# Operands of sixteen groups made over the MLP instead of twelve, in a fused attention, MLP and experts kernel

## The chip, the cores and the metric

The kernel runs on one core of a Trainium2 chip. The metric is the device time of one execution in microseconds (us); the time given for a kernel is the median of its runs.

## The reference, cut to what matters

```python
# attention, 4 batches x 8 heads x 576 x 64: x is 2304 tokens x 512
q_s = exp(q - max(q, -1)); q_s /= sum(q_s, -1)
k_s = exp(k - max(k, 2));  k_s /= sum(k_s, 2)
x = einsum(q_s, einsum(k_s, v))
# MLP, w_in 512 x 2048, w_out 2048 x 512
h = x @ w_in
x = maximum(0.01 * h, h) @ w_out
# gate
logits = x @ w_gate                    # 2304 x 8
P = exp(logits - logits.max())
for _ in range(8):                     # "balance"
    P /= P.sum(1, keepdims=True) + 1e-09
    P /= P.sum(0, keepdims=True) + 1e-09
    P *= N / E
# 8 experts, w1 512 x 1024, w2 1024 x 512 each
for e in range(8):
    out += P[:, e:e+1] * (maximum(x @ w1[e], 0) @ w2[e])
```

## The kernel before, in words

**Three stages.** Attention comes first, the MLP next (to some 499.5 us), then the experts. Every float32 operand is split in a high and a low part of type fp32r: `split` (L535, L536) casts the high part on ACT and subtracts it from the original on DVE, so each product is three matmuls, and PE carries nearly all of the time. Helper `mm` (L203) issues every matmul, so PE's rows are told apart by tile, not by line.

**The MLP** runs through 16 units of 128 hidden columns in 4 phases of 4 units; in a phase it takes 6 blocks of 384 tokens. A step is two half-steps: `first` (12 matmuls of 384 columns and the activation) and `second` (adds into the four banks y0 to y3, which are evicted at the end of a block by ACT, L239, or DVE, L241). There are 192 half-steps.

**The experts** run 3 superblocks of 768 tokens; in each, 32 groups of two 128-column units of the 8 experts' hidden layers (`NQ` = 32, `NG` = 96 in all). A group has seven half-steps t0 to t6 (`group`), one for each of the seven products with which Strassen's scheme replaces eight: banks `pa`, `pb`, `pc`, `pd` on PE, sums on ACT (L1000, L1025, L1027) and DVE (L944). The second matmul of groups 0 to `N0`-1 of superblock 0 is ordinary: `y_tile`, three tiles of 12 matmuls of 512 columns, tiles `e<-wb_t,xs`. All other groups do it by Strassen as well: `y_pass`, seven products of 6 matmuls of 384 columns, tiles `e<-xs,wb_t` and `e<-wa,wb_t`, with sums on ACT, POOL (L839, L840) and DVE (L845).

**Operands.** Strassen's scheme needs sums and differences of weight quarters, each split in high and low. Groups 0 to `N0`-1 make theirs while they run (`pair_sums` on POOL, `pair_w1` on ACT and DVE), and keep them in DRAM for the two later superblocks (`keep_w1` L559, `keep` L569: SP queue). Groups from `N0` on need theirs in DRAM before they start (`ring_load` L725 brings them in). Those are made during the MLP by `early_load` and `early_op`: list `early` holds two makings per pair of groups (w1 and w2), and `EARLY` names the half-step of each. One making: a load of 512 KB; two ACT casts; two DVE subtractions (L1206), of 128x768 and 128x1024 numbers; four POOL sums; stores of 768 and 1024 KB.

**Gate and balance.** In phase 4 of the MLP the finished blocks are transposed, split (`xs<-acc`, L364, L365) and multiplied with w_gate (tile `pg`). `balance` runs beside groups 0 to 5 of the experts: eight iterations, each with row sums and column sums on DVE, one tiny matmul with a matrix of ones (`pcs`) that adds the column sums over the partitions, a reciprocal `rc` (L423) and a scaling on DVE. `side_bank` gives `pcs` one of the banks y0 to y3, in turn.

**Borders.** At groups 32 and 64 a new superblock starts: its tokens need seven operands (`x_ahead`: four POOL subtractions of 128x768; `x_next`: splits). The output of a superblock is combined and transposed by `y_out` (tile `po`, copies L917, stores L919), which borrows banks; at the last superblock this is the end of the kernel. `op_split` makes the operands of the second matmul from the raw hidden activations, and each `sub_raw` one difference of them.

**What sets the order.** PE, ACT, POOL and SP run in the order in which the program issues (DVE's order is chosen by a scheduler). A generator's `yield` puts the rest of a task into the next half-step, `yield PE_NEXT` after that half-step's matmuls; `at(t, f)` starts a task at half-step t; `rest.append` puts a split at the start of the next half-step.

## Time and profile before

| | |
|---|---|
| median of 3 runs | 1960.81 us (1960.09 to 1961.35) |
| profiled execution, own time | 1959.87 us |
| its span | 1958.1 us |
| mean granted clock of TensorE | 0.994 |
| busy share of the span | PE 98%, PEld 95%, DVE 79%, ACT 43%, POOL 39% |
| DMA | 483.60 MB, mean 247 GB/s |

The span is the stretch of the profile from the first instruction to the last. PE is the matmul part of TensorE, PEld its weight loads (which lie beside the matmuls), DVE is VectorE, POOL is GpSimd, SP the engine whose queue starts most DMAs. Times in rows are in us from the start of the span, unless ns is said; `xN` is a count.

### The profile page before, as it was taken

Reading aid. Unit: us, or ns where it says so; the run is one execution under the profiler, and the core shown is the slowest. Engines: PE = TensorE matmul, PEld = TensorE weight load, DVE = VectorE, ACT = ScalarE, POOL = GpSimd, SP = SyncE. Lnnn points to the kernel's source line nnn. Section 1 sums busy time; section 2 is a strip of 40 time slices with the busy share of each in tenths; the row PEclk is TensorE's granted clock in tenths of the full one; section 3 lists DMA queues with packets and bytes.
Section 4 is the critical chain, followed back from the end, with each engine's and each line's share of the span. In section 5 each row is a group of like instructions: output and inputs, shape, how many; then the busy total and the mean of one; then the engine's idle time right before and its main releaser. Section 6 shows DMA issues by size and latency. Waiting matters only on the chain.

```text
span 1958.1 us, 31243 instructions
## 1 busy us (share of the span) xinstructions
PE 1925.3 (98%) x10835; PEld 1863.9 (95%) x10835; DVE 1550.6 (79%) x2285; ACT 836.5 (43%) x1528; POOL 758.5 (39%) x560
## 2 busy tenths in 40 slices
PE   7999999999999999999999999999999999999998
PEld 6999999999889999899999999999999999999998
DVE  7765768756788787779896898798898888888886
ACT  6744444444544444343344333333344433333333
POOL 4124323123323343126434445445633444544543
PEclk8999999999999999999999999999999999999999
DMA  6402768657688979888788988888888888887884
GB/s 249 166 14 67 248 205 272 209 175 236 244 282 286 325 285 331 286 315 258 233 276 262 326 275 260 270 261 260 254 256 247 275 261 261 259 260 235 278 260 153
DMA packets 279611, 483.60 MB, mean 247 GB/s; under 512 B 23536, under 2 KB 62848, under 8 KB 279424
## 3 DMA queue, kind: packets, MB, share of 16 engines
q1 hardware_dynamic: 278656, 480.04, 74.7%
q0 software_dynamic: 800, 1.57, 0.4%
q8 instruction: 88, 1.44, 0.3%
q14 instruction: 67, 0.55, 0.1%
HBM read 356.14 MB, written 128.52 MB: 248 GB/s over the span
## 4 chain that ended last, share of the span: by engine, by line
PE 62%; DVE 7%; issue 1%; ACT 1%; DMA 0%; SPq 0%; DVEq 0%; ACTq 0%
PE e L203 32%; PE pa L203 9%; PE pc L203 9%; PE pd L203 9%; PE pb L203 4%; DVE xs L536 1%; DVE c L944 1%; DVE mo_t L816 1%; DVE mo_t L802 1%; DVE wa L536 1%; DVE acc L845 1%; DMA mo_t<-in_w 0%; PE po L914 0%; ACT wa L535 0%; ACT acc L917 0%
## 5 line engine op out<-in xcount | busy, mean ns | idle before, releaser
L840 POOL TENSOR_TENSOR acc<-acc,acc 128x384 f32<-128x384 f32 x222 | 341.8, 1539 | 331.2 <-ACT acc L839 319.6
L203 PE MATMUL e<-xs,wb_t 128*128 128x384 f32 x1644 | 310.1, 334 | 1.4 <-ACT acc L917 1.4
L203 PE MATMUL e<-wa,wb_t 128*128 128x384 f32 x1548 | 290.5, 334 | 1.0 <-issue 0.9
L203 PEld LDWEIGHTS e<-xs,wb_t 128*128 128x128 f32 x1644 | 286.9, 188 | 2.3 <-ACT acc L917 2.2
L203 PEld LDWEIGHTS e<-wa,wb_t 128*128 128x128 f32 x1548 | 270.2, 188 | 1.5 <-issue 1.2
L816 POOL TENSOR_TENSOR mo_t<-mo_t 128x768 f32<-128x768 f32 x72 | 139.8, 1942 | 299.3 <-DVE mo_t L802 276.1
L839 ACT COPY acc<-e 128x384 f32<-128x384 f32 x222 | 106.3, 482 | 298.3 <-PE e L203 298.3
L536 DVE TENSOR_TENSOR wa<-mo_t,wa 128x768 fp32r<-128x768 f32 (+2 forms) x183 | 197.6, 1097 | 23.0 <-ACT wa L535 23.0
L203 PE MATMUL pa<-xs,wb_t 128*128 128x384 f32 x888 | 181.6, 339 | 3.0 <-ACT c L1000 2.9
L535 ACT CAST wa<-mo_t 128x768 fp32r<-128x768 f32 (+2 forms) x183 | 149.0, 839 | 79.0 <-DVE mo_t L816 57.2
L536 DVE TENSOR_TENSOR xs<-mo_t,xs 128x768 fp32r<-128x768 f32 x138 | 164.9, 1204 | 22.3 <-ACT xs L535 22.3
L203 PE MATMUL pc<-xs,wb_t 128*128 128x384 f32 x888 | 177.9, 334 | 1.5 <-ACT c L1025 1.5
L203 PE MATMUL pd<-xs,wb_t 128*128 128x384 f32 x888 | 178.4, 335 | 0.0
L845 DVE TENSOR_TENSOR acc<-e,acc 128x384 f32<-128x384 f32 x284 | 146.6, 548 | 34.8 <-PE e L203 19.8
L203 PE MATMUL e<-wb_t,xs 128*128 128x512 f32 x720 | 169.7, 393 | 1.2 <-DVE rc L423 1.2
L203 PEld LDWEIGHTS e<-wb_t,xs 128*128 128x128 f32 x720 | 135.7, 189 | 29.1 <-DVE rc L423 1.3
L203 PEld LDWEIGHTS pa<-xs,wb_t 128*128 128x128 f32 x888 | 154.1, 188 | 9.5 <-ACT c L1000 8.8
L535 ACT CAST xs<-mo_t 128x768 fp32r<-128x768 f32 x138 | 112.4, 836 | 109.8 <-DVE mo_t L816 70.3
L203 PEld LDWEIGHTS pc<-xs,wb_t 128*128 128x128 f32 x888 | 156.0, 188 | 2.1 <-ACT c L1025 2.1
L203 PEld LDWEIGHTS pd<-xs,wb_t 128*128 128x128 f32 x888 | 155.8, 188 | 0.3 <-DVE c L944 0.3
L816 DVE TENSOR_TENSOR mo_t<-mo_t 128x768 f32<-128x768 f32 x80 | 143.7, 1797 | 0.0
L802 DVE SCALAR_TENSOR_TENSOR mo_t<-c,mo_t 128x768 f32<-128x768 f32 (+1 forms) x152 | 126.6, 856 | 2.3
(178 smaller groups left out, 3226.9 us busy)
## 6 DMA issues: line engine op xcount, KB each, us to landing
wb_t<-d SPq DMA_DIRECT2D x1050, 256.0 KB, 3.4
d<-wa SPq DMA_DIRECT2D x20, 1792.0 KB, 9.9
d<-wb_t SPq DMA_DIRECT2D x56, 512.0 KB, 4.4
mo_t<-in_w SPq DMA_DIRECT2D x40, 512.0 KB, 7.4
raw<-in_wm SPq DMA_DIRECT2D x32, 512.0 KB, 5.4
d<-wa SPq DMA_DIRECT2D x15, 1024.0 KB, 5.1
d<-xs SPq DMA_DIRECT2D x13, 768.0 KB, 4.9
d<-wb_t SPq DMA_DIRECT2D x9, 1024.0 KB, 5.0
```

The source lines that it names most:

```text
L203: nc.tensor.matmul(o, a, b, start=start, stop=stop, **more)
L535: nc.scalar.copy(hi, a)
L536: return lambda: nc.vector.tensor_tensor(lo, a, r32(hi), op=ALU.subtract)
L802: nc.vector.scalar_tensor_tensor(o, p, 0.0, r, op0=ALU.max, op1=ALU.mult)
L816: eng.tensor_tensor(raw_q(o), raw_q(x), raw_q(y), op=ALU.subtract)
L839: nc.scalar.copy(t, bk[b])
L840: nc.gpsimd.tensor_tensor(c22, c22, t, op=ALU.add)
L845: return nc.vector.tensor_tensor(a, bk[b], a, op=ALU.add)
L944: add = lambda o, x, y: nc.vector.tensor_tensor(o, x, y, op=ALU.add)
```

## The change

`N0` falls from 20 to 16. Groups 16 to 19 of superblock 0 thereby take their operands from DRAM and do their second matmul by `y_pass`; 8 more makings run during the MLP (`EARLY` has 32 entries instead of 24: 11, 11 and 10 in phases 2, 3 and 4 instead of 8 each; in phase 4 they stand beside the half-steps after the gate's splits). With it:

- `side_bank` takes a bank that the running group's `y_tile` doesn't use, and `balance` issues some of its column sums later or earlier (`pcs4` one y tile later).
- The keeping of group 0's operands (`keep_w1(0)`, a DMA of 1792 KB) is issued at half-step `END`-3, not at the first half-step of group 0.
- `x_ahead`'s four POOL subtractions are issued one per two groups, from group `NQ`-8 on, not one after the other at `NQ`-6.
- At borders the splits `T3`, `B21`, `B22`, `T4` and a difference are issued one half-step later each; at the end `B11`, `T1`, `T2`, `T3` are placed anew in groups 94 to 96.
- `y_out` transposes in 4 banks of three tiles with copies of 384 columns and two DMAs of 384 rows each behind the last product, instead of 6 banks of two tiles with copies of 256 and one DMA each.

```diff
@@ -193,11 +193,11 @@
 
-    side_n = [0]
+    side_n = [0, 0]
 
...
         side_n[0] += 1
-        return ps_y.tile([P, 512], F32, tag=f"y{side_n[0] % 4}", name=name)
+        return ps_y.tile([P, 512], F32, tag=f"y{3 - side_n[1]}", name=name)
 
@@ -414,7 +414,7 @@
             yield
-            for _ in range((0, 2, 1)[min(it, 2)]):
+            for _ in range((0, 2, 1, 1, 2, 0, 1, 1)[it]):
                 yield
@@ -452,7 +452,7 @@
     NG = NSB * NQ
-    N0 = 20
+    N0 = 16
     KP = N0 // 2
@@ -664,7 +664,7 @@
     def stage_y(sb, n):
-        return acc[2 * NSB - 1 if sb == 0 else 1][:, n % 6 * 2 * P : (n % 6 + 1) * 2 * P]
+        return acc[2 * NSB - 1 if sb == 0 else 1][:, n * BLK : (n + 1) * BLK]
 
@@ -675,13 +675,8 @@
         x_parts[sb] = {"B11": b11, "T2": t2, "T1": t1, "T3": b12, "B21": b21, "B22": b22, "T4": t4}
-        nc.gpsimd.tensor_tensor(t1, b12, b11, op=ALU.subtract)
-        yield
-        nc.gpsimd.tensor_tensor(t2, b22, t1, op=ALU.subtract)
-        yield
-        nc.gpsimd.tensor_tensor(t4, b21, t2, op=ALU.subtract)
-        yield
-        nc.gpsimd.tensor_tensor(b12, b22, b12, op=ALU.subtract)
+        sub = lambda o, x, y: lambda: nc.gpsimd.tensor_tensor(o, x, y, op=ALU.subtract) and None
+        return sub(t1, b12, b11), sub(t2, b22, t1), sub(t4, b21, t2), sub(b12, b22, b12)
 
@@ -904,22 +899,24 @@
             yield
-        for th, quads in enumerate(((c11, cc), (dd, c22))):
+        for n, (a, th, h) in enumerate(((c11, 0, 0), (c22, 1, 1), (cc, 0, 1), (dd, 1, 0))):
+            if n % 2 == 0:
+                yield PE_NEXT
+            if sb == NSB - 1:
+                pt = bank(f"po{sb}_{dt}_{n}")[:, :BLK]
+            else:
+                pt = ps_y.tile([P, 512], F32, tag=f"y{(0, 2, 1, 3)[n]}", name=f"po{sb}_{dt}_{n}")[:, :BLK]
             for t in range(TB):
-                tt = th * TB + t
-                if tt % 2 == 0 and (tt < 4 or sb == NSB - 1):
-                    yield PE_NEXT
-                pt = (bank if sb == NSB - 1 else side_bank)(f"po{sb}_{dt}_{tt}")[:, : 2 * P]
-                for h, a in enumerate(quads):
-                    nc.tensor.transpose(pt[:, h * P : (h + 1) * P], a[:, t * P : (t + 1) * P], ident)
-                n = dt * 2 * TB + tt
-                o = stage_y(sb, n)
-                nc.scalar.copy(o, pt)
-                tok = 2 * sb * TB + tt
-                nc.sync.dma_start(
-                    (out if sb else ys_)[tok * P : (tok + 1) * P, :].rearrange("p (h t n) -> p h t n", h=2, t=2)[:, :, dt],
-                    o.rearrange("p (h n) -> p h n", h=2),
-                )
+                ts = slice(t * P, (t + 1) * P)
+                nc.tensor.transpose(pt[:, ts], a[:, ts], ident)
+            o = stage_y(sb, n)
+            nc.scalar.copy(o, pt)
+            tok = (2 * sb + th) * TB
+            k = 2 * h + dt
+            nc.sync.dma_start(
+                (out if sb else ys_)[tok * P : (tok + TB) * P, k * P : (k + 1) * P].rearrange("(t p) n -> p t n", p=P),
+                o.rearrange("p (t n) -> p t n", n=P),
+            )
 
@@ -988,11 +985,8 @@
                 y_steps(0)
-                if i == NG:
-                    rest.append(op_split(LG, "T3", raw_q(1)))
-                    rest.append(op_split(LG, "T2", raw_q(0)))
                 return
-            if i < N0 - 1:
+            if 0 < i < N0 - 1:
                 keep_w1(i)
@@ -1002,9 +996,6 @@
                 second_ops(0)
-            if ends(i - 1):
-                rest.append(op_split(eg - 1, "T3", raw_q(1)))
-                rest.append(op_split(eg - 1, "B21", raw_q(2)))
 
@@ -1030,12 +1021,16 @@
                 rest.append(op_split(eg, "T1", raw_q(0)))
+            if i == NG - 1:
+                rest.append(op_split(eg, "B11", raw_q(0)))
+            if ends(i - 1):
+                rest.append(op_split(eg - 1, "T3", raw_q(1)))
+                rest.append(op_split(eg - 1, "B21", raw_q(2)))
+
+        def t2():
+            drain()
             if ends(i - 1):
                 sub_raw(nc.vector, 2, 0, 2)
-                rest.append(op_split(eg - 1, "B22", raw_q(3)))
-
-        def t2():
-            drain()
             if i == N0:
@@ -1054,8 +1049,9 @@
             if ends(i - 1):
-                rest.append(op_split(eg - 1, "T4", raw_q(2)))
+                rest.append(op_split(eg - 1, "B22", raw_q(3)))
             if i == NG - 1:
+                sub_raw(nc.vector, 0, 1, 0)
                 rest.append(op_split(eg, "T1", raw_q(0)))
@@ -1081,6 +1077,8 @@
                 keep_w1(i)
+            if ends(i - 1):
+                rest.append(op_split(eg - 1, "T4", raw_q(2)))
 
@@ -1094,7 +1092,8 @@
                 if half == 0:
-                    rest.append(op_split(eg, "B11", raw_q(0)))
+                    if i < NG - 2:
+                        rest.append(op_split(eg, "B11", raw_q(0)))
                 elif not ends(i) and i < NG - 1:
@@ -1107,7 +1106,8 @@
                 if half == 0:
-                    sub_raw(nc.gpsimd if i < NG - 2 else nc.vector, 0, 1, 0)
+                    if i < NG - 2:
+                        sub_raw(nc.gpsimd, 0, 1, 0)
                 else:
@@ -1125,6 +1125,9 @@
                 rest.append(op_split(eg, "T4", raw_q(2)))
+            if i == NG - 1:
+                rest.append(op_split(eg, "T3", raw_q(1)))
+                rest.append(op_split(eg, "T2", raw_q(0)))
 
@@ -1185,7 +1188,7 @@
         else:
-            ks = (3, 2) if r < 26 else (3,)
+            ks = (3, 2) if r < 26 else (3,) if r < 39 else ()
         a = wa if ph % 2 else later["wb"]
@@ -1294,7 +1297,7 @@
     END = 2 * NS
-    EARLY = (53,57,62,67,72,78,83,94,98,103,107,112,116,121,126,131,149,153,157,161,165,169,173,177)
+    EARLY = (55,57,61,63,66,70,73,77,80,83,94,98,103,105,109,111,115,119,121,126,131,142,149,154,155,162,163,166,170,171,178,179)
     assert len(EARLY) == len(early)
@@ -1314,6 +1317,7 @@
     at(END - 4, second_load, 0)
+    at(END - 3, keep_w1, 0)
 
@@ -1353,14 +1357,16 @@
             at(t, x_next, i // NQ + 1)
-        if i % NQ == NQ - 6 and i < NG - 6:
-            at(t, x_ahead, i // NQ + 1)
+        if i % NQ == NQ - 8 and i < NG - 8:
+            for k, f in enumerate(x_ahead(i // NQ + 1)):
+                at(t + 14 * k, f)
         if i == NQ + 12:
...
                 at(t + 14 + th, y_done, th)
+        side_n[1] = i % 2
         for f in group(i):
...
             t += 1

```

Three places in the engines' orders show what the list above does.

ACT's order at the first border, groups 31 and 32 (`c1_32` is the first sum of group 32, `c2_..` its two later ones; `xs<-mo_t`, `wa<-mo_t` are splits of the hidden activations of the group before, `xs<-t4_1` an operand of the new superblock). Before:

```order
L535 CAST xs_85<-mo_t_3957 128x768
L535 CAST xs_85<-t4_1_8253 128x768
L1000 COPY c1_32_9090<-pa_32_9086 128x384
L535 CAST wa_86<-mo_t_3957 128x768
L535 CAST xs_85<-mo_t_3957 128x768
L1025 COPY c2_20_7434<-pc_32_9088 128x384
L1027 COPY c2_20_7434<-pd_32_9089 128x384
L535 CAST wa_86<-mo_t_3957 128x768 x2
```

and now:

```order
L535 CAST wa_86<-mo_t_4037 128x768
L535 CAST xs_85<-t4_1_8124 128x768
L994 COPY c1_32_9240<-pa_32_9236 128x384
L1016 COPY c2_16_7034<-pc_32_9238 128x384
L1018 COPY c2_16_7034<-pd_32_9239 128x384
L535 CAST wa_86<-mo_t_4037 128x768
L535 CAST xs_85<-mo_t_4037 128x768
L535 CAST wa_86<-mo_t_4037 128x768 x2
```

The two casts that stood between the copy of `pa` and the copies of `pc` and `pd` stand behind them.

PE's order at the fifth column sum of `balance` (`pd_4` is the last product of group 4, `e1_0` to `e1_2` are the y tiles of group 1). Before:

```order
L203 MATMUL pd_4_5336<-xs_85,wa_86 128x384 x6
L203 MATMUL e1_0_5426<-wb_t_1573,xs_85 128x512 x12
L203 MATMUL pcs4_5445<-cs4_5370,ones_75 128x8
L203 MATMUL e1_1_5458<-wb_t_1573,xs_85 128x512 x12
L203 MATMUL e1_2_5476<-wb_t_1573,xs_85 128x512 x12
```

and now:

```order
L203 MATMUL pd_4_5442<-xs_85,wa_86 128x384 x6
L203 MATMUL e1_0_5532<-wb_t_1573,xs_85 128x512 x12
L203 MATMUL e1_1_5551<-wb_t_1573,xs_85 128x512 x12
L203 MATMUL pcs4_5569<-cs4_5476,ones_75 128x8
L203 MATMUL e1_2_5582<-wb_t_1573,xs_85 128x512 x12
```

The sum has moved behind the second y tile.

SP's order where the experts start (`d1_0<-wa` is `keep_w1(0)`, L528 and L532 are `pair_load` and `second_load`, which bring the weights that the groups make operands from, `d2_15` is a store of the MLP's last making). Before:

```order
L1209 DMA d2_15_154<-wa_86 128x4x512
L528 DMA mo_t_3957<-in_w 128x2x512
L532 DMA mo_t_3957<-in_w 128x2x512
L528 DMA mo_t_3957<-in_w 128x2x512 x2
L559 DMA d1_0_107<-wa_86 128x7x512
L532 DMA mo_t_3957<-in_w 128x2x512
```

and now:

```order
L1212 DMA d2_15_154<-wa_86 128x4x512
L532 DMA mo_t_4037<-in_w 128x2x512
L528 DMA mo_t_4037<-in_w 128x2x512
L559 DMA d1_0_107<-wa_86 128x7x512
L528 DMA mo_t_4037<-in_w 128x2x512
L532 DMA mo_t_4037<-in_w 128x2x512
```

The keeping stands ahead of one more load instead of behind it.

## Rows read from the trace of the kernel before

**Rows 1.** The page, part 1: busy time of each engine.

```profile
PE 1925.3 (98%) x10835; PEld 1863.9 (95%) x10835; DVE 1550.6 (79%) x2285; ACT 836.5 (43%) x1528; POOL 758.5 (39%) x560
```

**Rows 2.** Windows view, phases 2 to 4 of the MLP: stretch, length, engines, PEclk, DMA share, GB/s.

```profile
188.00:287.40 99.40, 98.69 (x564) 98.43 (x564) 69.37 (x117) 44.11 (x82) 25.82 (x30) 1.00 0.68 220
287.40:388.90 101.50, 100.67 (x573) 99.74 (x573) 76.05 (x122) 45.23 (x81) 30.32 (x36) 1.00 0.74 241
388.90:499.50 110.60, 108.22 (x615) 101.95 (x614) 64.63 (x96) 50.18 (x87) 31.58 (x38) 1.00 0.59 191
```

**Rows 3.** Timeline of PE, two groups: start, us, engine, line, operation, out<-in.

```profile
782.40 8.36 PE L203 MATMUL e<-wb_t,xs 128*128 128x512 f32 x36
790.60 1.23 PE L203 MATMUL pa<-xs,wa 128*128 128x384 f32 x6
...
844.62 1.20 PE L203 MATMUL e<-xs,wb_t 128*128 128x384 f32 x6
...
851.90 1.20 PE L203 MATMUL pa<-xs,wb_t 128*128 128x384 f32 x6
```

**Rows 4.** Timeline of PE, start of the experts; in brackets the idle time before.

```profile
514.82 1.31 PE L203 MATMUL pa<-xs,wa 128*128 128x384 f32 x6 [1.58 <-ACT c L1000]
...
535.39 0.36 PE L203 MATMUL pcs<-cs,ones 128*128 128x8 f32 x2 [0.48 <-ACT wb_t L535]
...
563.73 0.39 PE L203 MATMUL pcs<-cs,ones 128*128 128x8 f32 x2 [1.89 <-DVE cs L414]
563.98 7.34 PE L203 MATMUL e<-wb_t,xs 128*128 128x512 f32 x24
...
578.69 5.64 PE L203 MATMUL e<-wb_t,xs 128*128 128x512 f32 x24
...
585.62 1.65 PE L203 MATMUL e<-wb_t,xs 128*128 128x512 f32 x6 [1.17 <-DVE rc L423]
```

**Rows 5.** Timeline of ACT, start of the experts.

```profile
511.88 1.78 ACT L535 CAST wa<-mo_t 128x1024 fp32r<-128x1024 f32 x2 [2.30 <-DMA d<-wa]
```

**Rows 6.** Windows view, while `balance` runs, and a part of it.

```profile
525.00:600.00 75.00, 71.45 (x354) 63.68 (x354) 64.40 (x133) 33.23 (x55) 24.06 (x22) 0.98 0.85 299
...
565.50:568.70 3.20, 3.20 (x9) 2.48 (x9) 1.80 (x4) 1.91 (x4) 0.00 (x0) 0.53 0.77 287
```

**Rows 7.** Waits view, the gate: waiter <- releaser: total us, times, longest.

```profile
PE pg L203 <- DVE xs L365: 2.2, 4, 0.7
```

**Rows 8.** Timeline of PE at the first border; POOL's first operation of `x_ahead` by source.

```profile
930.57 1.31 PE L203 MATMUL pa<-xs,wb_t 128*128 128x384 f32 x6 [1.22 <-ACT c L1000]
...
990.98 1.31 PE L203 MATMUL pc<-xs,wb_t 128*128 128x384 f32 x6 [0.75 <-ACT c L1025]
...
1026.46 0.79 PE L203 MATMUL e<-xs,wb_t 128*128 128x384 f32 x3 [0.68 <-ACT acc L917]
...
L678 POOL TENSOR_TENSOR acc<-acc,acc x2: 2572/2572/2573, 897.8 to 1371.9; 128x768 f32<-128x768 f32 x2
```

**Rows 9.** Timeline of PE, then of SP's queue, at the end.

```profile
1915.15 1.14 PE L203 MATMUL pa<-xs,wb_t 128*128 128x384 f32 x5 [0.50 <-ACT c L1000]
...
1935.18 1.12 PE L203 MATMUL e<-wa,wb_t 128*128 128x384 f32 x5 [0.91 <-issue]
...
1949.26 3.08 SPq L895 DMA_DIRECT2D out<-mo_t  x4
1952.44 2.54 SPq L919 DMA_DIRECT2D out<-acc  x4
```

**Rows 10.** Timeline of PE, phase 3 of the MLP.

```profile
309.10 0.79 PE L203 MATMUL y<-hh,wa 128*128 128x384 f32 x3 [0.72 <-DVE acc L241]
```

**Rows 11.** By source, one group each: count, min/median/max ns, first and last start.

```profile
L1206 DVE TENSOR_TENSOR wb_t<-rawe,wb_t x12: 951/1225/1228, 294.0 to 373.4; 128x1024 fp32r<-128x1024 f32 x9, 128x768 fp32r<-128x768 f32 x3
...
L816 DVE TENSOR_TENSOR mo_t<-mo_t x80: 942/1303/2619, 831.6 to 1935.9; 128x768 f32<-128x768 f32 x80
```

**Rows 12.** DMA issues: engine, operation, count, KB each, median us to landing.

```profile
d<-wb_t SPq DMA_DIRECT2D x9, 1024.0 KB, 5.0
```

## The prediction

> **What bounds the kernel now.** First the page's busy shares: TensorE's matmul part is busy 1925.3 us of a span of 1958.1 [rows 1]. The kernel can get faster in two ways only: fewer matmul columns, or fewer of the roughly 33 us in which PE stands. So I next read PE's own timeline for the gaps and asked of each what ended it. Some lie in the attention stage, which the change doesn't touch; the rest stand at the few places in rows 4, 7, 8, 9 and 10. Third, the windows view by stage: in phases 2 to 4 of the MLP, where the change puts new work, DVE is busy 69.37 of 99.40 us, 76.05 of 101.50 and 64.63 of 110.60, with the DMA engines at 0.68, 0.74 and 0.59 [rows 2]. This is the cover that has to hold. Idle time of other engines matters only where PE waits for them.
>
> **How a wait is priced.** Six matmuls of 384 columns show as 1.20 us, but in a dense row the next six begin 1.04 us on (the y_pass from 844.62 to 851.90 holds 42 such matmuls in 7.28 us, 0.173 each [rows 3]). A run's last 0.16 us overlaps the next run, so a gap of 1 us costs 1.16 us. I add that as a term of its own.
>
> **The change part by part.**
>
> *a. Four groups by Strassen.* A y_tile set starts at 782.40 and the next group's product at 790.60: 8.20 us. A y_pass takes 844.62 to 851.90: 7.28 us [rows 3]. Groups 16 to 19 save 4 x 0.92 = **3.7 us** of matmuls. They also drop their own making and keeping while the experts run, which is only cover there.
>
> *b. Start of the experts and balance.* PE stands 1.58 us at 514.82 for an ACT copy, 0.48 at 535.39 and 1.89 at 563.73 around column sums, and 1.17 at 585.62, where a y tile waits for the bank that the reciprocal rc still reads [rows 4]. The first goes back to an ACT cast that waited 2.30 us for a store of wa, that is keep_w1(0), to leave its buffer [rows 5]; SP had it behind a load that was itself waiting. The new order issues it one load earlier, ahead of the load that waited. The third is pcs4 waiting for its column sum; one y tile later (12 matmuls of 512 columns, about a third of 8.20, so 2.7 us) the sum is there. The last goes with the choice of a bank that no running y tile wants. The wait at 563.73 has an aftermath: the 24 matmuls behind it take 7.34 us where the same 24 take 5.64 at 578.69 [rows 4], and the window there has a granted clock of 0.53 [rows 6], that is the 1.2 GHz level, right after PE had stood. Without the wait I expect the full level: 1.70 us. All together 1.58 + 0.48 + 1.89 + 1.17 + 1.70 = 6.8. DVE is busy 64.40 of 75 us in this stretch [rows 6], so not every wait disappears: I take **5.0 us**, between 2 and 6.8.
>
> *c. Gate.* Four waits of pg for DVE splits, 2.2 us [rows 7]. The makings near them now stand beside the half-steps after the splits. I take **1.7**, between 0 and 2.2.
>
> *d. Borders.* At the first, 1.22, 0.75 and 0.68 us [rows 8]. The first wait follows POOL's block of four subtractions of 2.57 us each in x_ahead [rows 8], which delays POOL's other sums and so DVE and the cast ahead of the copy; spread over eight groups, each delays by one. The second is the copy of pc standing behind two casts, and the order shows those casts now behind it. The third is a borrowed bank of y_out. The second border repeats all three, 474 us on. 2 x 2.65 = 5.3; I take **4.9**, between 2.5 and 5.3 (if only the spread works).
>
> *e. End.* 0.50 and 0.91 us in the last groups, and a tail: four output stores take SP's queue 2.54 us to issue from 1952.44 while four of another shape take 3.08 [rows 9]. Two stand behind the last product instead of four: 2.54 / 2 = 1.3 saved, if issuing is what the tail waits for, and nothing if it is the landing. 0.50 + 0.91 + 1.3 = 2.7; I take **2.4**, between 0.5 and 2.7.
>
> *f. The hidden part of the waits.* Ten of those that go x 0.16 = **1.6 us**.
>
> *g. What the eight makings cost.* Each brings DVE 0.951 and 1.225 us [rows 11] = 2.18 us, so three more raise phase 2 to 75.9 of 99.40 us and phase 3 to 82.6 of 101.50; two more bring phase 4 to 69.0 of 110.60. No phase is full. Each moves 512 KB in and 1792 KB out, 2.36 MB; three in phase 3 are 7.1 MB in 101.5 us, 70 GB/s on top of 241. At the stretch's own ratio, 241 / 0.74 = 326 GB/s is a share of 1, so 311 is about 0.95. That is tight, but a store of 1024 KB lands in 5.0 us [rows 12] while 11 makings in 101.5 us come every 9 us. What can go wrong is local: at a block's end the evictions of y stand behind a making's DVE work, as once today, for 0.72 us [rows 10]. The low end is nothing, since 24 makings today leave hardly more than that; the high end is a full DVE half in PE's way for each, 8 x 1.225 = 9.8. Nearest is the low end; I take **2.5 us lost**, about one such wait more in each phase.
>
> A word on DVE and POOL working at once: the L816 subtractions, which run on both engines side by side, have a DVE time from 942 to 2619 ns for one shape, so one can be held 1.68 us. The subtractions of the makings don't show it: none is over 1228 where the median is 1225 [rows 11], so my price is 2.18 per making. The Trainium skill (SBUF — State Buffer, Who interferes with whom) says that a DVE instruction with two SBUF inputs and a GpSimd one that reads SBUF exclude each other and that the later one fully blocks. The L816 rows agree; the makings' rows don't show DVE as the later one. If the denser list made it so, 16 halves held 1.68 us each would add 27 us of DVE time, and term g would leave its range; this is the mechanism of rival C.
>
> **Sum.** -3.7 - 5.0 - 1.7 - 4.9 - 2.4 - 1.6 + 2.5 = -16.8 us. The profiled execution took 1959.87 (its span 1958.1 and 1.8 around it), so 1943.1; the median of the runs stands 0.9 above it, so **1944.0 us**. With every term at its good end the gain is about 22, at its bad end it is a loss of 1: 3.7 + 2 + 0 + 2.5 + 0.5 - 9.8.
>
> **The rivals.** *B: the waits move instead of going.* Balance and borders are places where DVE is nearly full (64.40 of 75 [rows 6]); a column sum that comes later makes rc later, which is the next thing a y tile or the next iteration waits for. For it: pcs4 moves by one tile and the later iterations follow without slack. Against: each wait of today is one late item, not a queue that never empties, as 578.69 shows a full pace between two of them. Then a, e and half of b, c and d remain: 3.7 + 2.4 + 5.8 + 0.8 - 2.5 = 10.2, and 4 if nothing but a's columns goes: 1950 to 1957.
>
> *C, the other side: the makings crowd the MLP.* Place: phases 2 and 3, where 22 makings now stand 2 to 5 half-steps of some 2.1 us apart (48 of them in a phase [rows 2]). If POOL's sums and DVE's halves collide so that evictions and activations come late in every one, PE waits per making. Without g the other terms are 19.3 us, so the kernel is slower by over 0.2% once g passes 23.2, which is 1.1 us of PE for each of those 22. Held 1.68 us each (the L816 spread [rows 11]) g is 37 us and the time 1979; at 1.1 to 1.6 us each it is 1965 to 1977. Against: the 16 makings there now cost a single visible 0.72 us wait in phase 3.
>
> *D: makings eat just what the rest brings*, with g at some 16 to 23: within 0.2%, 1957 to 1965.
>
> *E: part of the change doesn't act*, as when group 0's buffer is held by something behind the store, or the bank of the running y tile wasn't what held rc. That falls under B.
>
> **How the numbers follow.** The forecast (gain 11 to 23, 1937.5 to 1950) gets 0.66, B 0.19, D 0.07, C 0.08. No change means within 0.2%, 3.9 us, about what a measurement of this kernel can tell. Faster 0.85, same 0.07, slower 0.08. The range runs from 1937 to 1955: it leaves out C, D and B's end, and a few hundredths below.
>
> **What would show it.** In the new profile: groups 16 to 19 with y_pass rows of 7.3 us; no wait over 0.3 us at pcs4 and no stretch with a clock near 0.5 right after it; the first wait at the experts' start gone together with the ACT cast's wait for a store; at the borders the copies of pc ahead of the splits with PE going through; two stores behind the last product. In the MLP: DVE busy near 76, 83 and 69 us in phases of nearly today's length; DMA near 310 GB/s in phase 3. The forecast is wrong if phases 2 to 4 grow by more than 5 us together, or if PE shows waits for rc or for c at other times in balance and at the borders.

## The result, and the profile after

The changed kernel takes **1984.6 us** (median of 4 runs, 1982.76 to 1986.9) against 1961.08 before: a ratio of 1.0121, 95% interval 1.0109 to 1.0134. It is slower by 23.5 us, where 1944.0 was forecast.

The page, part 1, of the changed kernel, beside [rows 1]:

```profile
span 1983.7 us, 31544 instructions
PE 1932.6 (97%) x10859; PEld 1873.4 (94%) x10859; DVE 1571.0 (79%) x2299; ACT 842.0 (42%) x1528; POOL 783.3 (39%) x588
```

PE is busy 7.3 us more although there are fewer columns to multiply, and the part of the span in which it isn't has grown from 32.8 to 51.1 us. To see where the time went I cut the traces at the same points of the program: the starts of phases 2, 3 and 4 of the MLP (its 25th, 49th and 73rd activation), and the first ACT copy of groups 0, 4, 8, 32, 36, 60 and 68. A stretch of the clock as in [rows 2] won't do for this, because the changed kernel is later at each point and the same 99.40 us hold less of its work. The windows view of phases 2, 3 and 4, cut in this way, before (stretch, length, engines, PEclk, DMA share, GB/s):

```profile
181.81:283.80 101.99, 101.28 (x578) 100.70 (x577) 72.60 (x121) 45.30 (x84) 28.82 (x32) 1.00 0.66 214
283.80:386.14 102.34, 101.51 (x578) 100.58 (x577) 76.89 (x123) 45.96 (x82) 30.32 (x36) 1.00 0.73 239
386.14:502.69 116.55, 114.17 (x649) 107.91 (x648) 69.26 (x102) 54.11 (x94) 33.18 (x40) 1.00 0.56 181
```

and now:

```profile
183.11:295.26 112.15, 105.39 (x585) 101.23 (x584) 77.87 (x122) 49.47 (x90) 41.10 (x44) 1.00 0.77 255
295.26:409.68 114.42, 105.74 (x571) 103.29 (x570) 81.82 (x131) 48.59 (x88) 39.39 (x44) 0.96 0.81 263
409.68:530.21 120.53, 115.31 (x650) 109.65 (x649) 77.04 (x108) 59.67 (x100) 40.92 (x52) 0.99 0.71 241
```

The phases take 10.2, 12.1 and 4.0 us longer. DVE's busy time is close to what was forecast (77.87, 81.82 and 77.04 us against 75.9, 82.6 and 69.0), and the DMA share is 0.77 and 0.81 in phases 2 and 3, not 1. No engine other than PE is near full; they wait for one another.

The table has all runs; each column is the length of a stretch in us, for the kernel before as such and for the others as the difference from it ("rest" goes to the end of the span). Ahead of phase 2 the traces differ by up to 2 us, in the attention stage and phase 1, which no run touches; that is left out. One run of e2, 2106.53 us at a granted clock of 0.847, was slow and is left out of its time.

```
run                MLP   g0-4   g4-8  g8-32 g32-36 g36-60 g60-68   rest
before           320.9   51.1   67.5  364.8   66.0  352.0  122.1  431.9
after            +26.2   -2.0   +2.3   -4.8   +3.2   -1.2   +1.6   -1.0
e1_rest           -0.1   -1.6   +2.3   -0.0   +1.6   -1.3   +1.6   -1.1
e2_n16           +23.8   +0.0   -0.1   -3.2   -0.0   +0.1   -0.0   +0.4
e3_nostore       +24.4   -1.9   +0.5   -5.1   +3.1   -1.2   +1.6   -1.3
e4_nosums        +10.9   -2.0   +2.5   -5.1   +3.2   -1.2   +1.6   -1.1
e5_yield         +27.1   -2.3   +2.1   -4.6   +3.2   -1.2   +1.6   -1.3
e6_n18            +5.5   -0.0   -1.4   -0.3   -0.0   +0.1   +0.0   +0.0
e7_undo           -0.0   -1.6   +1.3   +0.4   -1.0   -1.3   -1.0   -1.1
e8_nosums_half    +5.5   -2.0   +2.5   -5.1   +3.2   -1.2   +1.6   -1.3
e9_best           +0.0   -1.5   +0.1   +0.3   -1.0   -1.2   -1.0   -1.1
e10_best2         +0.0   -1.6   -2.3   +1.0   -1.0   -1.2   -1.0   -1.1
e11_even         +20.2   -0.0   +0.1   -3.5   -0.0   +0.0   -0.0   +0.6
e12_nosub2       +10.5   -1.9   +0.8   -5.0   +3.0   -1.3   +1.6   -1.4
```

So 26.2 us are lost in the MLP, and the experts, where terms a, b and d to f promised 17.6 us, give back 1.9. Each row is one execution: the changed kernel and e2, with the same makings, differ by 2.4 us in the MLP, and the runs of the changed kernel by up to 4.1, so differences of 2 or 3 us there mean little. The waits view of the changed kernel says who waited in the MLP (waiter, releaser, total us, times, longest):

```profile
ACT wa L1208 <- POOL rawe L1228: 15.1, 4, 5.0
PE y L203 <- DVE acc L241: 14.5, 11, 3.2
...
ACT wb_t L1208 <- DMA d<-wb_t: 13.8, 3, 6.3
ACT wa L1208 <- POOL rawe L1226: 12.4, 4, 3.9
...
PE y L203 <- DVE hh L220: 3.5, 5, 1.2
```

PE waited once, 0.7 us, for an eviction by L241 before; now 11 times. And ACT's casts of the makings (L1208) wait for POOL's sums or for stores. One of these events, at 358.52, in the timelines of ACT, POOL, DVE and PE (in brackets the idle time before, and what ended it):

```profile
345.86 1.05 ACT L1208 CAST wb_t<-rawe 128x1024 fp32r<-128x1024 f32 x1 [2.83 <-DMA d<-wb_t]
...
348.12 0.82 ACT L1208 CAST xs<-rawe 128x768 fp32r<-128x768 f32 x1
...
354.30 1.05 ACT L1208 CAST wb_t<-rawe 128x1024 fp32r<-128x1024 f32 x1 [3.41 <-POOL rawe L1226]
...
350.78 0.74 POOL L1222 TENSOR_TENSOR rawe<-rawe 128x256 f32<-128x256 f32 x1 [9.05 <-DVE xs L1209]
...
353.52 0.74 POOL L1226 TENSOR_TENSOR rawe<-rawe 128x256 f32<-128x256 f32 x1
...
352.77 0.55 DVE L241 TENSOR_TENSOR acc<-y,acc 128x384 f32<-128x384 f32 x1
355.38 1.23 DVE L1209 TENSOR_TENSOR wb_t<-rawe,wb_t 128x1024 fp32r<-128x1024 f32 x1 [2.06 <-ACT wb_t L1208]
...
357.92 0.55 DVE L241 TENSOR_TENSOR acc<-y,acc 128x384 f32<-128x384 f32 x1
...
358.52 0.69 PE L203 MATMUL y<-hh,wa 128*128 128x384 f32 x1 [2.94 <-DVE acc L241]
```

Read it from the top. A cast waits 2.83 us for a store to leave its buffer. So the next making's first cast comes late (348.12), with it DVE's subtraction, and POOL's four sums, 350.78 to 354.26. The second cast, already at the head of ACT's order, waits for them 3.41 us. Its subtraction L1209 is at the head of DVE's order and waits too. The last of four evictions of y stands behind it: the third was issued at 352.77, the fourth at 357.92. PE needs that bank. DVE is not slow here, it stands still with work queued behind a late item.

There is a second price. The windows view around that wait and two others of 3 us:

```profile
358.50:362.00 3.50, 3.48 (x11) 3.48 (x12) 3.18 (x5) 1.70 (x4) 1.85 (x2) 0.50 0.96 365
397.70:401.50 3.80, 3.75 (x13) 3.58 (x14) 3.66 (x8) 0.87 (x2) 0.00 (x0) 0.60 0.93 273
473.00:476.80 3.80, 3.70 (x13) 3.73 (x14) 3.38 (x5) 0.83 (x1) 1.54 (x3) 0.57 1.06 404
```

After PE has stood, the granted clock is at 0.50 to 0.60, about its 1.2 GHz level, and matmuls start every 320 ns instead of 174. Measured from the start of one matmul to the start of the next over the MLP, 19 steps of more than 0.5 us hold 23.8 us beyond 174 ns each (6 steps and 4.7 us before), and 35 steps of 300 to 330 ns hold 5.1 us (none before): 19.1 + 5.1 = 24.2 of the 26.2.

### The profile page after: what moved, and what is told of

Same layout as the page of the kernel before. It is cut to its first block, busy times and chain, and to the rows that moved or that the text cites. A ratio compares the mean times of both kernels' runs of the same rounds, so it can differ in the third digit from the quotient of the medians.

```text
span 1983.7 us, 31544 instructions
## 1 busy us (share of the span) xinstructions
PE 1932.6 (97%) x10859; PEld 1873.4 (94%) x10859; DVE 1571.0 (79%) x2299; ACT 842.0 (42%) x1528; POOL 783.3 (39%) x588
## 3 DMA queue, kind: packets, MB, share of 16 engines
q1 hardware_dynamic: 291104, 495.12, 75.9%
## 4 chain that ended last, share of the span: by engine, by line
PE 64%; DVE 5%; issue 1%; ACT 0%; ACTq 0%; DVEq 0%
PE e L203 32%; PE pa L203 9%; PE pc L203 9%; PE pd L203 9%; PE pb L203 5%; DVE xs L536 1%; DVE mo_t L797 1%; DVE c L941 1%; DVE mo_t L811 1%; DVE wa L536 1%; PE po L911 0%; DVE acc L840 0%; DVE wb_t L536 0%; DVE acc L770 0%; DVE acc L771 0%
## 5 line engine op out<-in xcount | busy, mean ns | idle before, releaser
L835 POOL TENSOR_TENSOR acc<-acc,acc 128x384 f32<-128x384 f32 x234 | 355.4, 1519 | 342.9 <-ACT acc L834 330.6
L203 PE MATMUL e<-wa,wb_t 128*128 128x384 f32 x1680 | 318.5, 335 | 4.0 <-DVE wa L536 2.3
L203 PEld LDWEIGHTS e<-wa,wb_t 128*128 128x128 f32 x1680 | 293.2, 188 | 4.9 <-DVE wa L536 2.6
L203 PE MATMUL pa<-xs,wb_t 128*128 128x384 f32 x936 | 192.2, 340 | 0.2 <-ACT c L994 0.2
L203 PE MATMUL pd<-xs,wb_t 128*128 128x384 f32 x936 | 188.5, 335 | 1.4 <-DVE xs L536 1.4
L536 DVE TENSOR_TENSOR xs<-mo_t,xs 128x768 fp32r<-128x768 f32 x141 | 176.7, 1266 | 10.4 <-ACT xs L535 10.4
L535 ACT CAST wa<-mo_t 128x768 fp32r<-128x768 f32 (+2 forms) x183 | 148.6, 838 | 65.4 <-DVE mo_t L811 38.1
L811 DVE TENSOR_TENSOR mo_t<-mo_t 128x768 f32<-128x768 f32 x84 | 154.7, 1842 | 0.0
L797 DVE SCALAR_TENSOR_TENSOR mo_t<-c,mo_t 128x768 f32<-128x768 f32 (+1 forms) x160 | 138.8, 888 | 2.6
L203 PE MATMUL e<-wb_t,xs 128*128 128x512 f32 x576 | 134.5, 391 | 0.0
L203 PEld LDWEIGHTS e<-wb_t,xs 128*128 128x128 f32 x576 | 107.6, 188 | 21.8
```

Of the source, the lines that this page charges most:

```text
L203: nc.tensor.matmul(o, a, b, start=start, stop=stop, **more)
L535: nc.scalar.copy(hi, a)
L536: return lambda: nc.vector.tensor_tensor(lo, a, r32(hi), op=ALU.subtract)
L797: nc.vector.scalar_tensor_tensor(o, p, 0.0, r, op0=ALU.max, op1=ALU.mult)
L811: eng.tensor_tensor(raw_q(o), raw_q(x), raw_q(y), op=ALU.subtract)
L835: nc.gpsimd.tensor_tensor(c22, c22, t, op=ALU.add)
```

## The experiments

**Theory M**: the eight makings make the whole loss, in the MLP, because the chain of a making is late and stands in order ahead of the MLP's own work; the other edits only move their waits. Rivals are stated with each run.

**e1: all other edits without the makings.** `N0 = 20` and the old `EARLY` in the changed kernel.

```diff
-    N0 = 16
+    N0 = 20
-    EARLY = (55,57,61,63,66,70,73,77,80,83,94,98,...)
+    EARLY = (53,57,62,67,72,78,83,94,98,103,107,112,...)
```

> The changed kernel with N0 = 20 and the old EARLY list: all the other edits (balance, keep_w1(0), x_ahead, borders, y_out, end) without the eight makings. The trace of the changed kernel shows 26 us lost between the start of phase 2 of the MLP and the first group, and nearly nothing gained after it. Theory M (the makings alone make the loss, and the other edits move their waits on): 1957 to 1965 us. Rival L (the other edits are good for some 12 us as forecast and lose that only because the experts start late and crowded): 1944 to 1952.

1961.85 us against 1960.79; ratio 1.0007 (0.9997 to 1.0016), as theory M said; rival L falls. The edits gain 1.6 us at the experts' start, 1.3 ahead of the second border and 1.1 at the end, and lose 2.3 in balance and 1.6 at each border. Ahead of the first border the wait of 1.22 us shrinks to 0.19, but one of 1.08 comes in group 24, where the first of the spread subtractions now stands, so nothing is won.

**e2: the makings without the other edits,** in the kernel before.

```diff
-    N0 = 20
+    N0 = 16
-    EARLY = (53,57,62,67,72,78,83,94,98,103,107,112,...)
+    EARLY = (55,57,61,63,66,70,73,77,80,83,94,98,...)
```

> The kernel before with N0 = 16 and the new EARLY list, and none of the other edits. Theory M: the MLP is longer by 24 to 28 us and the four groups give 4 back, 1979 to 1986 us. Rival O (the loss in the MLP comes with the new order of the other edits, not with the count of makings): under 1970.

1981.84 us (median of three runs), ratio 1.0107 (1.009 to 1.0124): the MLP is 23.8 us longer, a little under what theory M said, and groups 8 to 32 are 3.2 shorter. The time is as theory M said; O falls.

**e3: a quarter of the makings without stores.**

```diff
         def put(o, j0, m):
+            if (i if kind == "w1" else 2 * i[0] + i[1]) % 4 == 1:
+                return
             nc.sync.dma_start(
```

> The changed kernel without the stores of 8 of its 32 makings, spread over the list (groups 17, 21, 25, 29; the readers take the operands of a neighbour, so this part of the result is left out). Loads, casts, subtractions and sums stay. Theory D (stores that leave their buffers late, at a DMA share near 1, hold ACT's casts and with them the activations): the 26 us in the MLP shrink to under 12, the time to under 1971. Theory P (the chain cast, subtraction, four POOL sums, second cast is too long for its place in ACT's order): the MLP stays within 5 us, the time over 1978.

1981.37 us in one run; the MLP still loses 24.4, as theory P said. A DMA share near 1 is not the cause: it went down from 0.77 to 0.69 and from 0.81 to 0.60 in phases 2 and 3 without effect. Whether ACT's waits for stores are a cause is not settled by this run, because they didn't shrink: its making casts waited 25.3 us for stores here and 21.2 in the changed kernel.

**e4: no POOL sums.**

```diff
-        nc.gpsimd.tensor_tensor(a22, a21, a22, op=ALU.add)
-        nc.gpsimd.tensor_tensor(a21, a11, a21, op=ALU.subtract)
...
```

> The changed kernel without the four POOL sums of each of the 32 makings (the operands made from them are left out of the result); loads, casts, subtractions and stores stay. Theory P: without the sums the second cast never waits, the 26 us shrink to under 8, the time to under 1967. Theory D: the waits of ACT for stores stay, 15 us or more of the 26 remain, the time over 1972.

1968.97 us in one run, between the two expectations: 15.3 of the 26.2 us go, 10.9 stay. The sums matter most of the parts left out so far, but not alone: the making casts' waits for stores rose from 21.2 to 38.1 us.

**e5: the second half a half-step later.**

```diff
         yield
         yield
+        if at_ not in (83, 131):
+            at_ += 1
+            yield
         o = early_out(4, at_ + 3)
```

> The changed kernel with one more half-step (2.1 us) between the sums of a making and its second half, for 30 of the 32. Theory P (the second cast stands too early in ACT's order, its subtraction too early in DVE's, and evictions and activations behind both): ACT's waits for POOL sums fall from 45 us to under 15, and the 26 us lost in the MLP to under 14; time under 1974. Rival W (the engines have no room, whatever the spacing, since DVE and the DMA engines are near full for stretches): the MLP stays within 5 us of the changed kernel's, time 1979 or more.

1984.26 us in one run: theory P as put here failed on the time. (The halves hold their buffers longer here and part of the operands comes out changed; the amount of work is the same.) ACT's waits for POOL fell from 45 to 9 us, as it said, but its waits for stores rose from 21 to 24 us in L1208 and from 6 to 9 in L163:

```profile
ACT wa L1208 <- DMA d<-wa: 19.4, 5, 7.4
ACT wb_t L1208 <- DMA d<-wb_t: 4.7, 4, 1.7
ACT wa L163 <- DMA d<-wa: 4.6, 1, 4.6
ACT wb_t L1208 <- POOL rawe L1226: 4.4, 2, 4.2
```

and the MLP as a whole is as long as ever, as rival W said. By phase it isn't. The windows view of phases 2 and 3, cut as above:

```profile
181.56:300.12 118.56, 107.64 (x585) 104.66 (x584) 80.20 (x122) 49.88 (x91) 42.55 (x44) 0.97 0.71 240
300.12:405.85 105.73, 101.79 (x571) 99.25 (x570) 80.57 (x126) 49.04 (x88) 37.92 (x44) 1.00 0.85 285
```

Phase 3 lost 12.1 us in the changed kernel and loses 3.4 here, with the same makings and DVE as busy. So there the place in the order, with what follows from it for the buffers, decides and not the amount of work, against rival W. In phase 2, where the waits of wa for stores stand (7.4 us in the changed kernel, 19.4 here), the loss grew from 10.2 to 16.6. The waits went to the next late item.

**e6: 28 makings.** The kernel before with `N0 = 18`; phases 2 and 3 as they were but for half-step 142, the rest in phase 4.

```diff
-    N0 = 20
+    N0 = 18
-    EARLY = (...,131,149,153,157,161,165,169,173,177)
+    EARLY = (...,131,142,149,152,155,158,161,164,167,170,173,176,179)
```

> The kernel before with N0 = 18: 28 makings, phases 2 and 3 of the MLP as before but for one making at their border (half-step 142), 11 in phase 4, three half-steps apart. If what matters is the spacing of makings in phases 2 and 3, the MLP is longer by 0 to 5 us and the two groups give back 1.6: 1958 to 1964 us. If the count decides (26 us for 8 makings, 3.3 each), the MLP is longer by 10 to 16: 1969 to 1975.

1968.97 us, ratio 1.0034 (1.0021 to 1.0047). The five runs lie in two clusters, two at 1965 and three at 1969, so the median is at the edge of the second expectation; the profiled execution, one of the lower two, took 1965.41 us. The MLP in it is 5.5 us longer, all in phase 4: 1.4 us per making, where eight cost 3.3 each. That is at the edge of the first expectation. What makes the other cluster 3.6 us slower is not known. In the traced run phases 2 and 3, as they were, cost nothing more. In phase 4 the gate pays:

```profile
PE pg L203 <- DVE xs L365: 4.7, 5, 1.8
```

against 2.2 in [rows 7].

**e7: old yields in balance, old border splits,** the rest as e1.

```diff
-            for _ in range((0, 2, 1, 1, 2, 0, 1, 1)[it]):
+            for _ in range((0, 2, 1)[min(it, 2)]):
...
             if half == 0:
                 second_ops(0)
+            if ends(i - 1):
+                rest.append(op_split(eg - 1, "T3", raw_q(1)))
+                rest.append(op_split(eg - 1, "B21", raw_q(2)))
...
```

> As the run with N0 = 20 and all the other edits, but with the old yields in balance (the new choice of banks stays) and the old places of the border splits. Theory M (the two edits only move their waits: column sum 5 and the second transpose of balance take the place of column sum 4, T4's late split takes the place of the copy of pc): groups 4 to 8 get 2 us back, groups 32 to 36 and 64 to 68 1.6 each, time 1955 to 1958 us. Rival (the waits at these places come from DVE's load and stay): 1960 to 1963.

1956.06 us, ratio 0.9977 (0.9968 to 0.9987), as theory M said, but not quite from where it said: the borders get back 2.6 each (from +1.6 to -1.0), balance only 1.0, for the wait at column sum 5 goes but that at column sum 4 is back. The second transpose still waits:

```profile
606.69 0.28 PE L434 MATMUL pT<-ident,pm 128*16 128x128 f32 x1 [2.47 <-DVE acc L771]
```

**e8: no sums, and every second making without stores:** e4, and

```diff
         def put(o, j0, m):
+            if (i if kind == "w1" else 2 * i[0] + i[1]) % 2 == 1:
+                return
```

> The changed kernel without the POOL sums of the makings and without the stores of every second making (left out of the result with what is made from them). Without the sums 11 of the 26 us in the MLP stayed, and ACT waited 38 us for stores. If stores hold ACT's casts, the 11 fall to under 4 and the time to under 1962; if DVE's and ACT's work of 32 makings alone costs it, they stay at 8 or more, 1966 or more.

1962.97 us in one run: 5.5 us stay of the 10.9 of e4, between the expectations. ACT's making casts now wait 15.0 us for stores instead of 38.1, so with the sums gone, stores do matter. What they cost beside the sums is not shown: e3 left their waits as long as they were.

**e9: e7 with the old banks.**

```diff
-        return ps_y.tile([P, 512], F32, tag=f"y{3 - side_n[1]}", name=name)
+        return ps_y.tile([P, 512], F32, tag=f"y{side_n[0] % 4}", name=name)
```

> As the run before with the old yields and old border splits (1956.1 us), and with the old turn of banks in side_bank as well. What stays of the change: keep_w1(0) earlier, x_ahead spread, y_out, the end. If the new choice of a bank makes the 2.47 us wait of the second transpose (its bank is one that DVE still empties for a y tile), groups 4 to 8 get 1 to 2.5 us back: 1953.5 to 1955.5 us. If that wait has another cause, it stays, 1956 or more.

1955.06 us, ratio 0.9968 (0.9956 to 0.9981); groups 4 to 8 get back 1.2, as the first expectation said. The transpose no longer waits, so the bank made that wait. Of the waits of the kernel before, that behind column sum 6 is back, and that at column sum 4 is there as in e7, with the slow 24 matmuls, as in [rows 4]:

```profile
563.11 0.39 PE L203 MATMUL pcs<-cs,ones 128*128 128x8 f32 x2 [1.90 <-DVE cs L414]
563.35 7.35 PE L203 MATMUL e<-wb_t,xs 128*128 128x512 f32 x24
...
585.08 3.02 PE L203 MATMUL e<-wb_t,xs 128*128 128x512 f32 x12 [1.24 <-DVE rc L423]
```

**e10: e9 with column sums 4 to 7 one tile later.**

```diff
-            for _ in range((0, 2, 1)[min(it, 2)]):
+            for _ in range((0, 2, 1, 1, 2, 1, 1, 1)[it]):
```

> The same with the old banks, and column sums 4 to 7 of balance each one y tile later than before (yields 0, 2, 1, 1, 2, 1, 1, 1), where the change takes the tile back at column sum 5. If the wait of 1.9 us and the slow clock after it only need one place more room, both go: 1.5 to 3.5 us less than the run above, 1951 to 1954 us. If the chain of DVE through the iterations is what is late, the wait comes back at a later sum or transpose: within 1 us of the run above.

1953.91 us, ratio 0.9965 (0.9953 to 0.9978): groups 4 to 8 are 2.3 us shorter than before the change, of which the groups behind lose 1.0 (0.3 in e9). Column sum 4 goes through, and one wait at column sum 6 takes the place of two:

```profile
563.19 0.28 PE L203 MATMUL pcs<-cs,ones 128*128 128x8 f32 x2
...
584.75 0.39 PE L203 MATMUL pcs<-cs,ones 128*128 128x8 f32 x2 [2.28 <-DVE acc L767]
```

The median is 1.1 us below that of e9, between the two expectations: most of the gain is there in the trace, but a wait did come back at a later sum, as the second said. It is faster than the kernel before by some 7 us, and than the changed one by 31; its runs overlap those of e9 and the traced one is the fastest of them, so the last step alone is seen in the trace only.

**e11: 32 makings spread evenly** in the kernel before with `N0 = 16`.

```diff
-    EARLY = (55,57,61,63,66,70,73,77,80,83,94,...)
+    EARLY = (53,56,60,63,66,70,73,77,80,83,94,98,101,105,108,112,115,119,122,126,131,142,149,152,155,158,161,164,167,170,173,177)
```

> The kernel before with N0 = 16 (1982.2 us with the list of the change) and the 32 makings spread as evenly as their windows allow: three to four half-steps apart, never two. If the pairs only two half-steps apart make the loss, the MLP's 24 us shrink to under 12: under 1971 us. If the number of makings in a phase makes it, they stay over 18: 1976 or more.

1979.29 us in one run; the MLP loses 20.2 instead of 23.8, as the second expectation said. The number in a phase makes most of it, the pairs two half-steps apart little. This run also bears on rival C of the prediction. None of its making subtractions was held; the longest took 1.227 us (by source, count, min/median/max ns):

```profile
L1206 DVE TENSOR_TENSOR wa<-rawe,wa x15: 947/1224/1227, 203.7 to 412.7; 128x1024 fp32r<-128x1024 f32 x11, 128x768 fp32r<-128x768 f32 x4
L1206 DVE TENSOR_TENSOR wb_t<-rawe,wb_t x15: 948/1224/1227, 304.7 to 391.0; 128x1024 fp32r<-128x1024 f32 x11, 128x768 fp32r<-128x768 f32 x4
```

**e12: no DVE subtraction in the second half of each making** (`m` is 3 in the first half, 4 in the second).

```diff
-            nc.vector.tensor_tensor(o[:, 1], a, r32(o[:, 0]), op=ALU.subtract)
+            if m == 3:
+                nc.vector.tensor_tensor(o[:, 1], a, r32(o[:, 0]), op=ALU.subtract)
```

> The changed kernel without the DVE subtraction of the second half of each making (that part of the operands is left out); loads, casts, sums and stores stay. If PE is hit through DVE's order (the subtraction waits for the late cast, and the evictions of y stand behind it), the 26 us in the MLP fall under 12, the time under 1971. If it is hit through ACT's order (activations behind the waiting cast), they stay at 18 or more, 1977 or more.

1966.5 us in one run; 10.5 of the 26.2 us stay, as the first expectation said. ACT still waits for POOL as long as before, 42 us, but PE's waits for evictions shrink from 14.5 us in 11 cases to:

```profile
PE y L203 <- DVE acc L241: 2.2, 3, 1.6
```

So POOL's lateness reaches PE mostly by way of DVE; of the waits that stay, 5.3 us are for ACT's activations (L218). DVE's work is less here as well (67.05 us in phase 2), so this run alone can't tell its order from its load. But the kernel before had more of it, 72.60, and not one wait of PE for DVE in that phase, so the amount alone is not what decides.

## Why the prediction was wrong

**g, the makings, is the step that failed.** It costed them at 2.5 us, with a high end of 9.8; they cost 23.8 alone (e2) and 26.2 with the rest. The step argued from busy shares, and these came out nearly as it said: DVE was to come to 75.9, 82.6 and 69.0 us in phases that it would not fill, and it was busy 77.87, 81.82 and 77.04 in phases that had grown. What the step left out is that a making is a chain over ACT, DVE, POOL, ACT, DVE and SP, with each link at a fixed place in an order that also carries the MLP's evictions and activations. A link that is late makes its engine stand, and everything behind it. Its high end, a DVE half in PE's way for each of the *eight*, was wrong twice: PE's longest wait for an eviction is 3.2 us (and an ACT cast's for a store 6.3), not 1.2, and a pause can be followed by matmuls at the lower clock, 5.1 us in all. The row that stood for the low end, one wait of 0.72 with 24 makings [rows 10], said that the old list fitted, not how much room it had left. That could have been asked of ACT in the same trace: its making casts waited 19.0 us in 12 cases for POOL's sums already before the change (44.9 us in 15 cases after it). The two largest:

```profile
ACT wa L1205 <- POOL mo_t L1223: 7.2, 4, 2.4
ACT wb_t L1205 <- POOL rawe L1225: 4.6, 3, 2.1
```

**Rival C** had the side, the place and the size right, with a chance of 0.08: 22.3 of the 26.2 us are lost in phases 2 and 3, over 1 us for each of its 22 makings, though PE waits for an eviction 11 times and not in every making. It overlooked that two of its gaps are 11 half-steps long (83 to 94, 131 to 142), which crowds the rest further. Its mechanism was half right: evictions do come late. It priced C by DVE instructions held by POOL ones, each by 1.68 us. The 64 making subtractions of the changed kernel took 1.72 us at most and 1.2 in the median of the larger shape, nearly as in [rows 11]; what they took beyond 0.951 and 1.225 us adds up to 2.5 us. In e11 not one was held, and the MLP still lost 20.2. The rule of the Trainium skill (SBUF — State Buffer, Who interferes with whom), by which a DVE instruction with two SBUF inputs and a GpSimd one that reads SBUF exclude each other, doesn't explain this loss: in this trace DVE was held these 2.5 us, and on POOL the four sums of a making take 3.57 us in the median where they took 3.56 before. The lateness is in the order. Nor did the DMA engines' busy share, which I counted up to 0.95 and which came to 0.81 in phase 3, decide (e3).

**a was right**: four groups by y_pass gave 3.2 us in e2, against 3.7. A y_pass in one of them runs from 839.91 to 847.19, 7.28 us as the term had it:

```profile
839.91 1.20 PE L203 MATMUL e<-xs,wb_t 128*128 128x384 f32 x6
...
847.19 1.20 PE L203 MATMUL pa<-xs,wb_t 128*128 128x384 f32 x6
```

**b failed in balance**, the second step that failed: 5.0 us were forecast, and e1 lost 0.7. keep_w1(0) gave 1.6 us, as the 1.58 of its wait said. The rest was rival B: PE at column sum 4 (`pcs4`, the fifth) goes through, but column sum 5 and the second transpose wait instead, each with slow matmuls behind it, and a column sum that comes later has less time to its next one where the change takes the tile back:

```profile
599.16 0.36 PE L203 MATMUL pcs<-cs,ones 128*128 128x8 f32 x2 [1.94 <-DVE cs L414]
...
632.75 0.28 PE L434 MATMUL pT<-ident,pm 128*16 128x128 f32 x1 [1.98 <-DVE acc L771]
```

The step looked at the waits to be removed, not at the slack of what follows, though the yields were in the diff. "A bank that no running y tile wants" was also read too kindly: the wait for rc went, but the bank was one that DVE had still to empty (e7 against e9). And the 1.70 us of slow matmuls behind the wait at 563.73 were counted as if they always came with such a wait; in e6 they don't (last section).

**d failed at the borders**, the third: 4.9 us were forecast, and e1 lost 1.6 + 1.6 and gained 1.3. x_ahead's spread gave 1.3 before the second border and, in e1, nothing before the first. The splits moved behind the copies took away the wait of pc (0.75) and the change in y_out that of the bank; but another wait of 0.69 us came, and T4's cast, issued a half-step later, then waits for DVE, and the last product of the y_pass needs it, here with a granted clock of 0.50 from 1026.52 on, which e1 doesn't have:

```profile
1024.07 0.83 ACT L535 CAST wa<-mo_t 128x768 fp32r<-128x768 f32 x1 [2.46 <-DVE mo_t L797]
1025.76 1.35 PE L203 MATMUL e<-wa,wb_t 128*128 128x384 f32 x5 [2.33 <-DVE wa L536]
```

With the old splits the border is 1.0 us shorter than before (e7). **e gave 1.0 to 1.1 us of its 2.4** (from group 68 to the end of the span): two stores issue in 1.00 us where four took 2.54, and the tail behind the last matmul fell from 5.6 to 4.3 us; but a new wait of 1.29 us stands at 1953.41, in a y_pass of the last groups, in place of the 0.50 and 0.91. **f** was right in the size of one wait: a wait of 1.98 delays the next start by 2.15; but most of the ten waits stayed or moved. **c** can't be told apart from g here; the waits for L365 are 1.0 us instead of 2.2, inside a phase that lost 4.0.

So a right price for g alone would not have saved the forecast: terms b, d, e and f were to bring 13.9 us, and e1, which has them without the makings, is no faster than the kernel before.

What stays open: which single delay starts the lateness in phase 2. Sums and DVE's halves each take part, and with the sums gone stores do too; without the sums and with half of the stores 5.5 us still stay. The runs that leave something out were made once each. Not tried were the sums with all stores left out, more buffers for the halves, or sums not made in place.

## What to carry to other kernels

Here the work hidden in another stage was not paid for in busy time but in places in each engine's order: before adding a chain over several in-order engines, ask how late each link may be until the stage's own work stands behind it, and count the chains that are in flight together. A wait that is removed has to be followed to the next use of the same chain; here the edits in balance and at the border splits only moved it, and trying them apart showed which were worth keeping. A stretch in which PE hardly waits tells nothing of its margin; the waits of the engines that carry the chain (19.0 us of ACT for POOL here) may.

## What was not expected of the hardware

A pause can cost more than its length, but it doesn't do so each time. Behind the three pauses of 2.9 to 3.2 us in the MLP the granted clock was 0.50 to 0.60 and matmuls of 384 columns started every 320 ns instead of 174: 9.3 us of pauses drew 5.1 us of slow matmuls. Pauses of 0.9 and 1.0 us at 243.97 and 272.42 left the clock at 1.00. In between, one execution differs from another. The pause of 1.89 us at 563.73 before the change had 24 matmuls in 7.34 us behind it [rows 4]; the same pause in e6, 1.92 us, has them at the full pace:

```profile
569.74 0.39 PE L203 MATMUL pcs<-cs,ones 128*128 128x8 f32 x2 [1.92 <-DVE cs L414]
569.98 5.73 PE L203 MATMUL e<-wb_t,xs 128*128 128x512 f32 x24
```

That is the -1.4 us of e6 in groups 4 to 8, where no edit of that run acts. Behind the pauses of 2.47 us in e7 (606.69) and 2.28 in e10 (584.75) the clock stayed at 1.00, too. So of the differences of 1 to 2 us in that column a part is this luck, among them the 2.3 us of e10.
